# Attention with a Fourier mixer on one core: the round trip of batch 0 on another queue, and the last second products by blocks

## The chip, the core and the metric

The kernel runs on one core of one Trainium2 chip. The core has a matrix engine (TensorE, PE in the profile, with PEld for its weight loads), three engines for elementwise work (VectorE, DVE; ScalarE, ACT; GpSimd, POOL), and SyncE (SP), which here only issues transfers. Transfers can also be issued from the queues of ACT and of POOL. The metric is the time of one execution on the device, in microseconds (us).

## The reference

Inputs are q, k and v with 4 batches, 8 heads, 768 positions and 64 channels, and two weights, 512 x 2048 and 2048 x 512. What is computed, cut to what matters:

```python
scores = scale * q @ k.T - slope[h] * dist      # kept: the first 8 keys, and the last 96 keys
a = softmax(where(keep, scores, -1e9))
x = (a @ v), heads side by side                 # (4, 768, 512)
mixed = real(fft over positions, then over channels of x)
u = x + mixed
un = (u - mean(u)) / sqrt(var(u) + 1e-6)
out = u + maximum(un @ w_ch1, 0) @ w_ch2
```

## The kernel before

**Chunks.** Each batch has 768 rows, which come out of the Fourier mixer as six groups of 128 rows (row r, r + 6, ...). Two groups, a pair in `PAIRS`, make a chunk, so there are three chunks per batch and twelve in all (c = 0 to 11). Heads go in pairs (hp = 0 to 3).

**Attention.** `load` brings q, k, v of a head pair; for batches 0 and 1 they are cast (`cast_qk`, `cast_v0`) and transposed on PE (`trans`, tiles pt, copied out to qkT), and v is laid out by products with an identity (`v_place`, pvp). `score` makes the score bands (sc), ACT takes exp (ex), `v_global` and `glob` treat the eight global keys (pvg, pgl, eg), and `av` makes the weighted sums (pav), normalized by DVE into x.

**Bounce.** The residual needs x with its rows in the other grouping. `bounce` writes x to a scratch tensor in DRAM (xd) and reads it back as XR (xr). Batch 0 does it in two halves of the columns, and waits for both before the read. All of these transfers are issued from ACT's queue.

**Mixer.** `fold_3` (batch 0) or `fold_s` and `fold_d` combine rows and columns of x by symmetry on DVE; `y_unit` (py) is the transform over positions, `mirror` makes reversed copies on POOL (ww, rev), and `u_unit` (pu) is the transform over channels. DVE adds XR into u with the row sums (line 980), scales the sums to minus the mean (sm, line 984), and ACT or DVE makes un (lines 995, 997). `nt_unit` transposes un on PE (ptu), from chunk 7 on by a transposing transfer.

**The two products.** `ph_unit` makes one eighth of the first product of a chunk (16 blocks of 128, two at a time; 8 matmuls of 256 columns each), and ACT or DVE applies the maximum with 0 into hT. `pg_unit` makes a quarter of the second product for one row group t (4 matmuls of 512 columns), and after the fourth DVE scales it by the row's rstd and adds it to u, which SP stores.

**Who sets the order.** Nothing here is written out in order. The class `Plan` walks a model of the engines: every operation is given with what it needs, its cost and the engines that could do it; the planner places the earliest next, and picks from four streams of PE work (mixer, attention, ph, pg). What it emits is then each engine's fixed program. So a change of a need, a buffer, a bank or a queue moves other instructions too. Times on tokens for transfers are set in `Plan.emit`.

PSUM banks: two double banks "xx", and two more, C and D, that serve batches 0 and 1. When all users of C and D are done (the token CD), their space goes to the rings of ph and pg, two banks each. No ph can start before that. Weights are loaded by `wload` from POOL's queue, cast on the way, in eight pieces of 512 KB as stored. Before the first product there are twelve products of zeros (pz).

## Time and profile before

| | |
|---|---|
| median of 8 runs | 276.66 us (275.5 to 278.07) |
| profiled execution | 275.5 us |
| its span, first to last instruction | 273.7 us |
| mean granted clock of TensorE | 0.998 |
| PE, DVE, ACT, POOL busy | 257.1, 153.2, 148.6, 61.2 us |
| ph products (128x256) | 768, busy 94.3 us |
| pg products (128x512) | 384, busy 89.8 us |
| weight pieces, issue to landing (median) | 11.9 us |
| v of a head pair, issue to landing (median) | 7.3 us |
| writes xd of batch 0, issue to landing (median of four) | 7.0 us |
| read xr, issue to landing (median) | 4.7 us |

A row of the timeline gives the start, the duration, the engine, the line, the operation with output and inputs, how many, and in brackets the idle time before it and what ended it. Matmuls are pipelined, so that the duration of a group counts from the first start to the last end, and the pace of one is the distance from start to start. PEclk is the clock that TensorE was granted, in tenths. Where an engine waits for several things, the bracket names what came last.

### The profile page before, as it was taken

To read this page: it belongs to the slowest core of one execution; us is meant where nothing else is said; L and a number is where in the kernel's file an instruction comes from. 1 tells how busy PE (TensorE), PEld (TensorE's weight loads), DVE (VectorE), ACT (ScalarE), POOL (GpSimd) and SP (SyncE) were. 2 spreads that over 40 slices of the span, in tenths; PEclk is the share of its full clock that TensorE was granted. 3 is DMA by queue.
4 is the path that set the end of the run, shared out by engine and by line. 5 is a ranking of instruction groups with operands and counts; after the bars stand their busy time and mean duration, and the time that the engine had idled before them with its cause. 6 is when DMAs were issued, how large, how long until landed. Compare 5 with 4: busy or idle time off the path is not lost.

```text
span 273.7 us, 5973 instructions
## 1 busy us (share of the span) xinstructions
PE 257.1 (94%) x2420; PEld 171.1 (63%) x2420; DVE 153.2 (56%) x316; ACT 148.6 (54%) x257; POOL 61.2 (22%) x127
## 2 busy tenths in 40 slices
PE   8698899589789999999999999999999999999994
PEld 3344548459567864777486466568887677767441
DVE  4565954973885415665378968567896224211121
ACT  1486666594766633697772066998453263535000
POOL 1445195830002502413110023032004101010000
PEclk9999999999999999999999999999999999999999
DMA  7999999996935597968957994415341241210122
GB/s 205 291 293 312 351 271 232 207 198 124 261 118 170 126 156 169 234 140 140 220 137 181 179 327 93 106 38 41 84 150 41 77 79 40 77 41 31 48 77 78
DMA packets 75742, 42.01 MB, mean 153 GB/s; under 512 B 32834, under 2 KB 71746, under 8 KB 75714
## 3 DMA queue, kind: packets, MB, share of 16 engines
q1 hardware_dynamic: 66914, 31.14, 47.7%
q0 software_dynamic: 4224, 4.19, 9.3%
q10 hardware_dynamic: 4576, 6.29, 7.9%
q8 instruction: 19, 0.31, 0.5%
q14 instruction: 9, 0.07, 0.1%
HBM read 31.92 MB, written 9.44 MB: 151 GB/s over the span
## 4 chain that ended last, share of the span: by engine, by line
PE 76%; DVE 7%; SPq 5%; ACT 4%; DMA 3%; issue 2%; POOL 1%; ACTq 1%; DVEq 0%; POOLq 0%
PE pg L1087 30%; PE ph L1064 29%; PE py L881 5%; SPq L365 4%; PE pu L961 3%; PE sc L552 3%; PE pav L680 3%; DMA w<-in_q_dram 3%; ACT ex L575 2%; PE pav L669 1%; DVE sm L984 1%; DVE qkT L521 1%; ACT un L1004 1%; POOL ww L929 1%; PE ptu L1036 1%
## 5 line engine op out<-in xcount | busy, mean ns | idle before, releaser
L1064 PE MATMUL ph<-unT,w 128*128 128x256 f16 x768 | 94.3, 273 | 2.2 <-DVE hT L1071 2.2
L1087 PE MATMUL pg<-w,hT 128*128 128x512 f16 x384 | 89.8, 379 | 0.0
L1064 PEld LDWEIGHTS <-w 128*128 128x128 f16 x768 | 72.7, 98 | 19.1 <-issue 6.1
L1070 ACT ACTIVATE hT<-ph 128x512 f16<-128x512 f32 x75 | 44.8, 597 | 49.0 <-PE ph L1064 48.0
L1087 PEld LDWEIGHTS <-hT 128*128 128x128 f16 x384 | 36.9, 98 | 36.9 <-issue 0.8
L1096 DVE SCALAR_TENSOR_TENSOR u<-pg,sm,u 128x512 f32<-128x512 f32 x24 | 18.0, 750 | 57.2 <-PE pg L1087 57.1
L575 ACT ACTIVATE ex<-sc 128x992 f16<-128x992 f32 (+2 forms) x24 | 20.9, 926 | 13.9 <-PE sc L552 8.2
L1071 DVE TENSOR_SCALAR hT<-ph 128x512 f16<-128x512 f32 x21 | 14.5, 690 | 15.4 <-PE ph L1064 15.3
L572 ACT ACTIVATE er<-sc 128x992 f16<-128x992 f32 (+2 forms) x24 | 21.6, 924 | 1.6 <-PE sc L552 1.5
L1011 POOL TENSOR_SCALAR sm<-sm 128x2 f32<-128x2 f32 x12 | 3.1, 255 | 84.1 <-ACT un L1004 83.9
L369 ACT ACTIVATE qk<-qs 128x384 f16<-128x384 f32 (+1 forms) x31 | 14.5, 528 | 8.9 <-DMA qkT<-qk 8.5
L980 DVE SCALAR_TENSOR_TENSOR u<-pu,xr 128x512 f32<-128x512 f32 x24 | 15.6, 687 | 5.6 <-PE pu L961 2.9
L587 DVE TENSOR_TENSOR ex<-er,mk 128x992 f16<-128x992 f16 (+2 forms) x24 | 14.8, 626 | 5.2 <-ACT er L572 4.9
L552 PE MATMUL sc<-qkT 64*128 64x256 f16 (+1 forms) x192 | 17.1, 262 | 0.6 <-DVE qkT L521 0.6
L680 PE MATMUL pav<-v,ex 128*128 128x65 f16 x352 | 16.4, 193 | 1.0 <-ACT ex L575 1.0
L1004 ACT ACTIVATE un<-un 128x512 f16<-128x512 f16 x24 | 14.9, 621 | 3.9 <-DMA unT<-un 2.9
L680 PEld LDWEIGHTS <-ex 128*128 128x128 f16 x352 | 15.3, 97 | 2.3 <-issue 1.7
L929 POOL COPY ww<-zy 128x512 f16<-128x512 f16 x16 | 9.3, 611 | 31.2 <-PE py L881 31.2
L995 ACT ACTIVATE un<-u,sm 128x512 f16<-128x512 f32 x12 | 8.5, 717 | 14.0 <-DVE sm L984 11.0
L552 PEld LDWEIGHTS <-qkT 64*128 64x128 f16 x192 | 5.7, 94 | 14.9 <-issue 12.4
L481 POOL COPY kG<-qkT 64x8 f16<-64x8 f16 x32 | 9.5, 298 | 24.1 <-DMA qkT<-qk 13.3
L898 DVE CAST zy<-py 128x512 f16<-128x512 f32 (+1 forms) x9 | 8.3, 928 | 10.8 <-ACT zy L896 6.4
(103 smaller groups left out, 297.1 us busy)
## 6 DMA issues: line engine op xcount, KB each, us to landing
out_dram<-u SPq DMA_DIRECT2D x24, 256.0 KB, 2.0
w<-in_moe_w_ch_dram POOLq DMA_DIRECT2D x8, 512.0 KB, 11.9
qs<-in_q_dram SPq DMA_DIRECT2D x9, 384.0 KB, 4.4
qs<-in_k_dram SPq DMA_DIRECT2D x9, 384.0 KB, 5.2
u<-in_v_dram SPq DMA_DIRECT2D x8, 384.0 KB, 7.3
xr<-xd ACTq DMA_DIRECT2D x4, 768.0 KB, 4.7
qs<-in_v_dram SPq DMA_DIRECT2D x16, 192.0 KB, 3.9
w<-in_q_dram SPq DMA_DIRECT2D x4, 384.0 KB, 6.6
```

Of the source, the lines that this page charges most:

```text
L369: A(d, s, AF.Copy)
L552: nc.tensor.matmul(pa[:, s, c0:c0 + cw], TT[n][lo:lo + 64, 1, i * P:(i + 1) * P], TT[n][lo:lo + 64, 0, i * P:i * P + cw], start=(b > 1), s ...
L572: A(mine(), cut(pa), AF.Exp, 0.0, 0.125)
L575: A(cut(expst[hp][:, :, g * 512:g * 512 + (384 if g == 2 else 512)]), cut(pa), AF.Exp, 0.0, 0.125)
L587: VT(o, mine(), m, op=ALU.mult)
L680: nc.tensor.matmul(po[:, jj, hh * 65:(hh + 1) * 65], lhsT, v16[b % 2][:, i, h, 0:65], start=(jp == 0 and a == 0), stop=(a == len(ops) - 1) ...
L980: V.scalar_tensor_tensor(u[:, a].rearrange("p (n r) -> p n r", r=4), pu[:, a].rearrange("p (r n) -> p n r", r=4), 1.0, XR[b][:, rr].rearra ...
L1004: A(x, x, AF.Square, accum_out=MV[c][:, a, 2:3])
L1064: nc.tensor.matmul(ph[:, a * CH:(a + 1) * CH], W1[0][:, d, jb * P:(jb + 1) * P], UNT[c][:, d, :], start=(d == 0), stop=(d == ND - 1))
L1070: pl.later([("ACT", act(512), lambda: A(dst, ph, AF.Relu)), ("DVE", dve(512), lambda: V.tensor_scalar_max(dst, ph, 0.0))], [], e, [("h", c ...
L1087: nc.tensor.matmul(pg, HT[c][:, jb, t * P:(t + 1) * P], W2[0][:, jb, :], start=(jb == 0), stop=(jb == NJ - 1))
L1096: V.scalar_tensor_tensor(UT[c][:, t, :], pg, MV[c][:, t, 3:4], UT[c][:, t, :], op0=ALU.mult, op1=ALU.add)
```

## The change

- Batch 0's bounce is issued from SP's queue. The four v of batch 1 are loaded after its read has been issued (the token xi), three of them into the buffers qs.
- For batch 0, u is added by row group: each of the two adds is an operation of its own, and its row sum is scaled by ACT and not by DVE, so that un of one group does not wait for the other.
- The second product of chunks 8 to 11 is done by blocks of two by two. With the four blocks of hT (row group by half of the inner size) and of w2 (half of the inner size by half of the columns), sums of blocks are formed on DVE, and seven products of blocks take the place of eight. The sums over w2 are made once (`w2_sums`, into the buffers of the exps, after batch 3's last use of them), those over hT per chunk (`s_sums`, into the mask's buffer and in place). Seven blocks of 8 matmuls of 256 columns, and five adds to u, per chunk.
- Fourteen products of zeros follow the products of v of head pair 0, ten precede those of head pair 1.
- The weight pieces wait for the cast of k of batch 1's last head pair in place of v's second, and the planner's numbers for some landings are changed. The transpose of chunk 0 may use banks C and D.

```diff
+    LAND = {("xw", 0, 0): 33.0, ("xw", 0, 1): 37.0, ("xr", 0): 43.0}
...
-            self.tok[o] = end + lat if dma else (end + lat, eng)
+            self.tok[o] = max(end + lat, self.LAND.get(o, 0.0)) if dma else (end + lat, eng)
...
+    def vat(n):
+        return ("u", min(n, HP)) if n < HP or n == 2 * HP - 1 else ("qs", 2 + n - HP)
...
-            pl.later([("SP", 0.55, run)], free("u", n), 0.0, [("ld", n, 2)], lat=1.7, dma=1.45)
+            pl.later([("SP", 0.55, run)], free(*vat(n)) + [("xi",)] * (n >= HP), 0.0, [("ld", n, 2)], lat=1.7, dma=1.45)
...
+            idle = lambda k: [nc.tensor.matmul(pv[:, 1, 3 * P:4 * P], EG[:, 0:P], EG[:, 0:P], start=True, stop=True) for _ in range(k)]
+            if n == 1:
+                idle(10)
...
+            if n == 0:
+                idle(14)
...
-        on, eng = "ACT", nc.scalar
+        on, eng = ("ACT", nc.scalar) if b else ("SP", nc.sync)
...
+            def add1(a):
+                if a == 0:
+                    UT[c] = buf("u", HP + 1 + c, [P, 2, Dm], FP32, 2)
+                    MV[c] = wk.tile([P, 2, 4], FP32, tag="sm", name=f"sm_{c}", bufs=6)
+                V.scalar_tensor_tensor(UT[c][:, a].rearrange("p (n r) -> p n r", r=4),
+                                       pu[:, a].rearrange("p (r n) -> p n r", r=4), 1.0,
+                                       XR[b][:, PAIRS[pr][a]].rearrange("p (n r) -> p n r", r=4),
+                                       op0=ALU.mult, op1=ALU.add, accum_out=MV[c][:, a, 0:1])
...
+                for a in range(2):
+                    pl.later([("DVE", dve(512) + 0.06, lambda a=a: add1(a))],
+                             [("xr", b)] + (free("u", HP + 1 + c) if a == 0 else [("us", c, 0)]), e, [("us", c, a)],
+                             ([("free", "xr", b)] + CD(b, ring)) * a, ring=ring if a else None)
+                    pl.later([("ACT", 0.2, lambda a=a: A(MV[c][:, a, 1:2], MV[c][:, a, 0:1], AF.Copy, 0.0, -SC / Dm))],
+                             [("us", c, a)], 0.0, [("u", c, a)], rank=0)
...
+    def w2_sums(i):
...
+            VT(W2T(1)[:, k0], b22, b12, op=ALU.subtract)
+            VT(W2T(3)[:, k0], b12, b11, op=ALU.subtract)
+            VT(W2T(0)[:, k0], b22, W2T(3)[:, k0], op=ALU.subtract)
+            VT(W2T(2)[:, k0], b21, W2T(0)[:, k0], op=ALU.subtract)
...
+    def s_sums(c):
...
+        def s1():
+            VT(new(0), block(1, 0), block(1, 1), op=ALU.add)
+        def s3():
+            VT(block(1, 0), block(0, 0), block(1, 0), op=ALU.subtract)
+        def s2():
+            VT(new(1), SX[c, 0], block(0, 0), op=ALU.subtract)
+        def s4():
+            VT(new(2), block(0, 1), SX[c, 1], op=ALU.subtract)
...
+    def pg_units(c):
...
+        PG.append((h0 + ws, ("pg",), p1))
+        PG.append((h1 + [("s", c, 1)], ("pg",), p45))
+        PG.append(([("s", c, 2), ("ra", c, 0)], None, p6))
+        PG.append(([("s", c, 4), ("rd", c, 0)], None, p32))
+        PG.append(([("s", c, 3), ("ra", c, 1)], None, p7))
...
-            needs = [("vc", 5), ("free", "w1", 0)] if i == 0 else [("wl", 3), ("free", "w2", 0)] if i == 4 else [("wl", i - 1)]
+            needs = [("qk", 7, 1), ("free", "w1", 0)] if i == 0 else [("wl", 3), ("free", "w2", 0)] if i == 4 else [("wl", i - 1)]
...
+            if c >= CS:
+                s_sums(c)
+                pg_units(c)
+                continue
```

In `pg_units`, p1, p6 and p7 each make one block product into one bank (pgA), p45 and p32 two each into the other (pgD). Before p6 and p7 write pgA again, the add that reads it must be done (ra), and p32 waits in the same way for the add that reads pgD (rd).

## The prediction

> **What bounds the kernel now.** I read the page's busy shares and slices first, then the windows of 10 us, then the chain that ended last, and at each hole in TensorE the timelines of the engines that it waits for.

> ```profile
> PE 257.1 (94%) x2420; PEld 171.1 (63%) x2420; DVE 153.2 (56%) x316; ACT 148.6 (54%) x257; POOL 61.2 (22%) x127
> PE   8698899589789999999999999999999999999994
> PEclk9999999999999999999999999999999999999999
> ```

> TensorE (PE) is busy for 94% of the span at full granted clock; the low digits lie in the first third.

> ```profile
> 40.00:50.00 10.00, 9.10 (x117) 7.58 (x115) 5.07 (x9) 5.01 (x8) 6.89 (x12) 1.00 1.01 210
> 50.00:60.00 10.00, 7.51 (x122) 4.77 (x122) 8.54 (x21) 8.87 (x18) 5.36 (x11) 1.00 1.22 199
> 70.00:80.00 10.00, 7.82 (x57) 5.39 (x56) 8.74 (x16) 6.38 (x12) 0.00 (x0) 1.00 0.77 227
> 100.00:110.00 10.00, 10.00 (x56) 5.00 (x55) 4.53 (x10) 3.48 (x8) 2.05 (x5) 1.00 0.87 166
> ```

> Columns: stretch, length, busy time of PE, its weight loads, DVE, ACT, POOL, then clock, DMA share, GB/s. Summed over all windows PE lacks 12.9 us before 100 us, nothing between 100 and 260, and 3.7 us after its last product. So two things count: products taken away after 92 us come off the end one for one, and ahead of it only a hole in PE that closes counts.

> The last part of the chain (start, us, what):

> ```profile
> 243.07 1.75 PE ph L1064 x16
> 252.65 17.28 PE pg L1087 x80
> 269.95 0.75 DVE u L1096
> ```

> A pg product of 512 columns takes 17.28/80 = 0.216 us, a ph product of 256 columns 1.75/16 = 0.109. The end is pure PE work, one DVE add and a store.

> The holes, first at 25 to 30 us:

> ```profile
> 23.53 2.31 ACTq L719 DMA_DIRECT2D xd<-x  x2
> 25.89 2.56 ACT L575 ACTIVATE ex<-sc 128x992 f16<-128x992 f32 x3 [2.40 <-DVE vG L611]
> 26.94 0.34 PE L680 MATMUL pav<-v,ex 128*128 128x65 f16 x6 [0.48 <-ACT ex L575]
> 29.21 0.23 PE L669 MATMUL pav<-vG,eg 128*128 128x130 f16 x1 [0.35 <-ACT eg L645]
> ```

> ACT's queue spends 2.31 us issuing the first half of the bounce; the exps of head pair 3, whose scores lie ready, come late, and PE waits for the banks they hold. The name vG in the bracket is only the last semaphore; what held ACT is the line above. Next, at 48 us:

> ```profile
> 48.32 2.77 DVE L984 TENSOR_SCALAR sm<-sm 128x2 f32<-128x2 f32 x1
> 49.91 1.17 DVE L443 CAST v<-pvp 128x384 f16<-128x384 f32 x1
> 48.20 0.74 POOL L1183 DMA_DIRECT2D w<-in_moe_w_ch_dram  x1
> 48.94 0.62 POOL L929 COPY ww<-zy 128x512 f16<-128x512 f16 x1
> 49.49 0.74 POOL L1183 DMA_DIRECT2D w<-in_moe_w_ch_dram  x1
> 50.22 0.83 POOL L414 CAST er<-u 128x768 f16<-128x768 f32 x1
> 51.90 0.62 PE L1036 MATMUL ptu<-ident,un 128*128 128x128 f16 x8 [2.49 <-ACT un L995]
> ```

> The tiny sm scaling, 0.17 us elsewhere, takes 2.77 and ends at 51.09, as POOL's unbroken run does (51.05). un waits for it, and the transpose of un is what PE stands on.

> **The change, part by part.** I walk the instruction order of the changed kernel with durations of the one profiled execution. It took 275.5 us with a span of 273.7, so 1.8 lies outside; the median of the eight runs, 276.66, stands 1.2 above it. I sum against 275.5 and add the 1.2.

> *Block form (chunks 8 to 11).* Removed: 4 x 32 = 128 products of 512, 128 x 0.216 = 27.65 us. Added: 4 x 7 x 8 = 224 of 256, at ph's 0.109, 24.50. That is -3.15 on PE. The ph row already loads new weights for each 256 columns at this pace, so that is in the price. DVE gains per chunk four sums of 128x1024 (0.61 start to start at L750/L751) and three more adds, 4 x (2.4 + 1.5) = 15.6 us over the last 60 us, where DVE is busy 8 to 47%. The eight sums over w2 (8 x 0.61 = 4.9 us) go ahead of batch 3's last normalization and fold: from the last pav, sums 4.9, x 0.9, fold and zy 6.1, one add 0.7, g1 1.8, hence w ready 13.6 us later; ahead of py PE has 11 ph (9.6) and 6 quarter pg (5.2), 14.8. Hidden by 1.2 us; without that cover they would cost up to 4.9. At the very end, from the last ph product: relu to +0.75, two sums to +2.0, the add that frees a pg bank to +2.8, where PE wants it at +2.6. With semaphores, +0.3. The last add then waits 0.1 at most. Net -2.85. The bound above: all five products of chunk 11 wait in turn for a DVE step, some +2.

> *Batch 0's bounce on SP.* Its five issues leave ACT and follow t1x, whose issue ends at 29.44. The first half's issue (rows ready at 23.5) is then at 29.5, the second's when x is done, near 31.2. Landing of such writes is 3.9 to 7.5 us; without the four v loads beside them (6.44 us of issue at 29.54 in before) I take 4.5: 37. The read lands 4.2 to 4.9 later, 42, and its first user (u of chunk 0) comes at 44. On ACT, two qk casts (0.75 each) move in from POOL; still the exps of head pair 3 end near 27.4 in place of 28.35, and eg at 28.0 in place of 29.16. So pav_4_1 starts at 28.1, not 29.21: -1.1. The next qkT copies are earlier by 0.9, and the third goes to ACT, so that DVE has the last fold done at 36.4 in place of 38.2; the PE waits of 0.36 and 0.41 for qkT go. py starts near 36.8 (39.25), with one score group less ahead of it (0.84). PE's holes from 25 to 45 us: before 0.61 + 0.48 + 0.52 + 0.35 + 0.36 + 0.41 = 2.7, after about 1.0. That is -1.7.

> *v of batch 1 behind the bounce; weights earlier.* v4 to v7 are issued at 37.5 to 40 in place of 29.5 to 36; four pvp, their evacuations and all of batch 1's pav move back, and the first ph units come forward in their place, at about 52 (61.46 before). The eight weight issues come at about 36.8 to 43, in one run. Behind them on POOL stand the mirrors (ww, rev) and v's casts: eight by 0.75 ends near 43, rev at 44.7, where pu of chunk 1 needs it at 45.7; the last ww at 47, needed at 48. v4 must be in by 48. With xr (768 KB) and the four v sharing the DMA engines with the weights at half of some 290 GB/s (the rate from 10 to 20 us), v4 lands near 45, v7 near 53 (cast needed by 60). Nothing in before shows v beside weights: at best they land in 4 us, at worst after the last weight, 26 us behind the first issue as in before (39.8 to 66.1). I take the even split, for which the nearest row is xr itself, issued at 40.41 between the first weights and landed within 4.9.

> [...]

> *u by row groups.* The three sm scalings on DVE become six ACT scalings of 128x1 (nearest row: a 128x1 accumulator read, 0.19; up to 0.3 each; 1.2 to 1.8 us on ACT), and un of the first row group can start under the second's add. The 2.77 us stall has no instruction left to sit in.

> [...] But un on DVE is a tensor_scalar too and now comes at 47.3, in POOL's run of ww, kG and two casts (46.3 to 48.8). [...] I take 0.5.

> PE holes from 45 to 62: before 0.31 + 2.49 + 0.2 + 0.17 + 1.08 = 4.25. After: ph must wait until bank D's last user, pvp of v4, is evacuated behind ACT's squares and scalings (51.1 to 52.3, 1.2), 0.1 for ptu of chunk 2, 0.5 for the lock, 0.6 for v casts on POOL: 2.4. That is -1.8. What is late next is ACT, which from 48 to 61 has 12 us of work in 13.

> *70 to 92 us.* Before: 1.40 + 0.78 + 0.43 = 2.6, the first two waits for relus on DVE behind the fold while ACT does mk for 3.86 us. After, eight ph of chunk 0 are already done; ACT's mk comes in pieces, the relus have pg units beside them, py finds w ready 1 us early. I keep the mirror wait and some slack, 0.8: -1.8.

> *Zero products.* 14 x 0.057 = 0.8 us after pvp of v0, 10 x 0.057 = 0.6 before the next pvp: they fill the holes of 0.84 and 0.73 at 11.4 and 13.0. pt and sc there take the durations of later ones (0.83, 0.59), so there is no slow clock to cure: 0, between -0.1 and +0.2.

> **Sum.** -2.85 - 1.7 - 1.8 - 1.8 = -8.15. A walk by hand misses short waits; I add back 0.65, about the three shortest of before (0.31, 0.2, 0.17). -7.5: 268.0 for an execution like the profiled one, **269.2** against the median.

> **The rivals.**

> *Waits change places (0.20).* ACT and DVE are at 85 to 89% from 50 to 60 us and get ph's relus on top; the holes before 92 us only move and the block form alone is left: 276.66 - 2.85 = 273.8. For it speaks ACT's 12 us in 13; against it, that before leaves ACT idle for 23 of the first 60 us and the queue stall there goes for certain.

> *Nothing (0.08).* The w2 sums lose their 1.2 us of cover (copies 20% slower than L750) and the end waits for DVE three times: 3 us back, while the first part only moves: 276.4. The profile speaks for a busy DVE only from 140 to 160, not after 210.

> *v starves behind the weights, slower (0.12).* pvp of v4 stands in PE's order ahead of every ph. If the engines do not share evenly, v4 lands with the last weight, 36.8 + 26 = 63; with its cast and pvp PE goes on at 64 in place of 50: +14 - 7.5 = +6.5, 283.2. It decides from a landing at 56.5 on (7.5 us later than the 49 at which PE would feel it), that is 19 us after issue, where v took 7.3 in the median. For it: DMA share was above 1.2 through the weights from 46 to 64. Against: xr's 4.9.

> *No new waits at all (0.05).* Without my 2.2 us of allowances: 267.

> **How the numbers follow.** 0.55 for the sum, whose own range is 266.5 to 272, 0.20, 0.08, 0.12 and 0.05 as above. Faster by over 0.5% (1.4 us, about what a measurement of this kernel can tell): 0.55 + 0.20 + 0.05 = 0.80; within it 0.08; slower 0.12. The range of 266.3 to 276.6 leaves out the starved case and the best tail.

> **What would show it.** Right: 256 pg products of 512 columns in place of 384, and 224 of 256 columns at 0.109; no PE hole over 1.3 us between 25 and 92; no DVE scaling of 2 us; exps of head pair 3 without ACT's 2.4 us gap; xr landed before pu of chunk 0 ends; PE whole from 92 to the end but for 0.3. Wrong: PE standing at pvp of v4 or on ww/rev behind the weight issues; py of batch 3 waiting for DVE; PE waiting in the last 9 us for adds by more than 1 us.

## The result, and the profile after

The changed kernel takes 273.73 us (median of 20 runs, 270.62 to 276.72), the kernel before 276.85 in all runs (275.29 to 279.38). The medians give a gain of 3.1 us where 7.5 were forecast. The ratio is 0.9865, with a 95% interval of 0.9842 to 0.9887; it leaves out five runs that lie more than 1.5% above the fastest, and so stands for 3.7 us. The profiled execution took 273.71 us, with a span of 271.9.

Where the 4.5 us went is read in the same order as before. First the page's busy shares and slices:

```profile
PE 256.8 (94%) x2540; PEld 182.1 (67%) x2540; DVE 172.1 (63%) x349; ACT 153.3 (56%) x267; POOL 57.7 (21%) x123
PE   8798899679999899999999999899999999999994
PEclk9999999979999999999999999999999999999999
```

PE is as busy as before (256.8 and 257.1 us), though it has fewer products to make. The 7 near 70 us has become a 9. The eighth slice (47.6 to 54.4 us) has gone from 5 to 6 only, the ninth from 8 to 7, and in the ninth the granted clock falls to 7 tenths. The windows say how much (columns as before: stretch, length, PE, its weight loads, DVE, ACT, POOL, clock, DMA share, GB/s):

```profile
40.00:50.00 10.00, 10.00 (x122) 7.90 (x120) 5.81 (x14) 5.87 (x12) 6.75 (x15) 1.00 1.16 248
50.00:60.00 10.00, 5.66 (x63) 3.16 (x61) 4.55 (x10) 5.29 (x15) 2.53 (x4) 0.83 1.20 216
60.00:70.00 10.00, 9.40 (x121) 7.42 (x118) 3.02 (x5) 7.25 (x15) 2.53 (x4) 1.00 1.05 183
70.00:80.00 10.00, 10.00 (x148) 8.77 (x144) 7.84 (x16) 3.71 (x8) 2.39 (x3) 1.00 0.63 135
```

One window of 10 us lacks 4.34 us of PE and runs at 0.83 of the clock. PE's timeline in it:

```profile
50.84 0.36 PE L436 MATMUL pvp<-er,ident 64*64 64x128 f16 x12
56.14 0.40 PE L436 MATMUL pvp<-er,ident 64*64 64x128 f16 x12 [4.25 <-POOL er L420]
56.48 1.89 PE L1090 MATMUL ph<-unT,w 128*128 128x256 f16 x8
58.16 1.00 PE L553 MATMUL sc<-dist,sid 128*128 128x480 f16 x2
59.10 0.58 PE L563 MATMUL sc<-qkT 64*128 64x240 f16 x4
59.61 0.67 PE L1062 MATMUL ptu<-ident,un 128*128 128x128 f16 x8
60.12 1.91 PE L1090 MATMUL ph<-unT,w 128*128 128x256 f16 x16
...
67.22 0.36 PE L436 MATMUL pvp<-er,ident 64*64 64x128 f16 x12 [0.60 <-POOL er L420]
```

The products of v5 wait 4.25 us for POOL's cast, those of v7 0.60. The first ph stands behind those of v5 in PE's order, not only behind those of v4. Between the two waits eight ph take 1.89 us in place of 1.03, and two sc 1.00 in place of 0.58: the granted clock, 1.00 up to 56 us, is 0.59 from 56 to 58, 0.56 from 58 to 60, and 1.00 again from 60 on. From 56.14 to 60.12 stands work that takes about 2.45 us at full clock (each group at its usual pace), so some 1.5 us are lost on top. The casts on POOL say what they wait for:

```profile
49.96 0.82 POOL L420 CAST er<-qs 128x768 f16<-128x768 f32 x1 [2.11 <-DMA qs<-in_v_dram]
55.27 0.83 POOL L420 CAST er<-qs 128x768 f16<-128x768 f32 x1 [4.48 <-DMA qs<-in_v_dram]
60.89 0.82 POOL L420 CAST er<-qs 128x768 f16<-128x768 f32 x1 [3.70 <-DMA qs<-in_v_dram]
66.35 0.82 POOL L420 CAST er<-u 128x768 f16<-128x768 f32 x1 [3.58 <-DMA u<-in_v_dram]
```

So v4 to v7 land near 49.9, 55.2, 60.8 and 66.3, one about every 5.5 us. SP issued them from 38.17 on:

```profile
38.17 5.07 SPq L371 DMA_DIRECT2D qs<-in_v_dram  x3
43.29 6.20 SPq L371 DMA_DIRECT2D u<-in_v_dram  x1
```

All four issues had ended by 49.5, and v7 landed some 17 us after that. The DMA view for 44 to 60 us splits the two queues (packets, MB, share); q0 carries the weights from POOL, q1 carries v:

```profile
q0 software_dynamic: 2286, 2.26, 83.3%
q1 hardware_dynamic: 2292, 1.15, 35.3%
```

The packets are equal in number, 2286 and 2292, and unequal in size: 2.26 MB / 2286 is 989 bytes, 1.15 MB / 2292 is 502, both in the mean. In 16 us that is 141 GB/s for the weights and 72 for v. In every 3 us from 43 to 64 us the counts of the two queues lie within 3 of each other. So v's packets went through all the time, some 143 in each us (2292 in 16): what set v's landing behind 49.5 was not the late issue but this pace.

Most of the rest stands as forecast; a wait of 0.80 us at 173.73 (sc, for ACT) does not. ACT's exps of head pair 3 no longer stand behind the bounce:

```profile
24.45 0.98 ACT L586 ACTIVATE ex<-sc 128x992 f16<-128x992 f32 x1
...
26.06 1.66 ACT L586 ACTIVATE ex<-sc 128x960 f16<-128x960 f32 x2
```

They end at 27.7 (28.45 before). The 2.77 us of the sm scaling are gone, un on DVE takes 0.48 at 48.11 and 49.12, and xr is in before u needs it:

```profile
48.11 0.48 DVE L1023 TENSOR_SCALAR un<-u,sm 128x512 f16<-128x512 f32 x1
```

The end of the chain of waits is still pure PE, now with block products at 1.75 us for 16, which is the pace of the ph beside them:

```profile
251.06 1.75 PE ph L1090 x16
252.81 1.75 PE pgD L1194 x16
```

### The profile page after: what moved, and what is told of

Its sections match the earlier page's. It is cut to its first block, busy times and chain, and to the rows that moved or that the text cites. A ratio compares the mean times of both kernels' runs of the same rounds, so it can differ in the third digit from the quotient of the medians.

```text
span 271.9 us, 6257 instructions
## 1 busy us (share of the span) xinstructions
PE 256.8 (94%) x2540; PEld 182.1 (67%) x2540; DVE 172.1 (63%) x349; ACT 153.3 (56%) x267; POOL 57.7 (21%) x123
## 4 chain that ended last, share of the span: by engine, by line
PE 76%; DMA 13%; SPq 4%; DVE 2%; POOL 2%; issue 1%; ACT 1%; POOLq 0%; DVEq 0%
PE ph L1090 29%; PE pg L1113 21%; DMA u<-in_v_dram 11%; PE pgD L1194 5%; PE pav L690 4%; PE pgA L1194 4%; PE sc L563 3%; PE py L891 3%; SPq L371 3%; PE pu L971 3%; DMA xd<-x 2%; PE pav L679 1%; PE sc L558 1%; PE pt L526 1%; PE ptu L1062 1%
## 5 line engine op out<-in xcount | busy, mean ns | idle before, releaser
L1096 ACT ACTIVATE hT<-ph 128x512 f16<-128x512 f32 x75 | 44.6, 596 | 46.8 <-PE ph L1090 46.6
L1113 PE MATMUL pg<-w,hT 128*128 128x512 f16 x256 | 60.2, 379 | 0.0
L598 DVE TENSOR_TENSOR ex<-er,mk 128x992 f16<-128x992 f16 (+2 forms) x24 | 14.8, 626 | 12.0 <-ACT er L583 11.9
L375 ACT ACTIVATE qk<-qs 128x384 f16<-128x384 f32 (+1 forms) x33 | 15.4, 522 | 11.5 <-DMA qkT<-qk 8.4
L1122 DVE SCALAR_TENSOR_TENSOR u<-pg,sm,u 128x512 f32<-128x512 f32 x16 | 11.9, 747 | 8.8 <-PE pg L1113 8.8
L1030 ACT ACTIVATE un<-un 128x512 f16<-128x512 f16 x24 | 14.8, 620 | 1.0 <-DMA unT<-un 1.0
L1021 ACT ACTIVATE un<-u,sm 128x512 f16<-128x512 f32 x13 | 9.2, 719 | 10.6 <-DVE sm L994 10.5
L465 POOL CAST v<-qs 128x768 f16<-128x768 f32 x8 | 7.4, 928 | 35.8 <-DMA qs<-in_v_dram 35.8
L906 ACT ACTIVATE zy<-py 128x1024 f16<-128x1024 f32 (+1 forms) x11 | 9.0, 827 | 10.6 <-PE py L891 10.2
L990 DVE SCALAR_TENSOR_TENSOR u<-pu,xr 128x512 f32<-128x512 f32 x18 | 11.7, 687 | 4.3 <-PE pu L971 4.3
```

The lines of the kernel that those rows point to most:

```text
L375: A(d, s, AF.Copy)
L598: VT(o, mine(), m, op=ALU.mult)
L1030: A(x, x, AF.Square, accum_out=MV[c][:, a, 2:3])
L1096: pl.later([("ACT", act(512), lambda: A(dst, ph, AF.Relu)), ("DVE", dve(512), lambda: V.tensor_scalar_max(dst, ph, 0.0))], [], e, [("h", c ...
L1113: nc.tensor.matmul(pg, HT[c][:, jb, t * P:(t + 1) * P], W2[0][:, jb, :], start=(jb == 0), stop=(jb == NJ - 1))
```

## The experiments

**Issue v between the writes and the read.** The theory was that v is late because it lands beside the weights. This edit sends v before them; the rival was that the wait moves to xr.

```diff
-                      lat=1.7, dma=2.4 if b else 2.6)
+                      lat=1.7, dma=2.4 if b else 2.6,
+                      then=None if b or n == 0 else (lambda t: pl.tok.__setitem__(("xi",), pl.t["SP"])))
...
-        pl.later([(on, 0.5, rd)], ..., dma=3.8 if b else 2.4, then=None if b else (lambda t: pl.tok.__setitem__(("xi",), pl.t["SP"])))
+        pl.later([(on, 0.5, rd)], ..., dma=3.8 if b else 2.4)
```

> The four v of batch 1 are issued between the writes and the read of batch 0's bounce, where SP stands idle from 32.3 to 37.7 us and the DMA share falls to 0.12, and not behind the read. Theory (v shares the DMA engines with the weights and lands 12 to 23 us after issue; PE stands 4.25 us at a pvp, then runs some 4 us at half clock, and stands 0.6 us again): v lands by 40, no PE hole over 1.5 us from 45 to 70, clock 1.00 throughout; 6 us under the changed kernel, near 267. Rival (the waits only change place: xr now lands behind v, or ACT is the bound): u of chunk 0 waits for xr, and 3 us or less are gained, 271 or more.

Measured: 272.47 us (270.57 to 276.0), ratio 0.9812 [0.976, 0.9865]. The profiled execution is its slowest, 276.0. In it v4 is cast at 39.48, and no pvp waits; but xr, issued at 38.6 behind four v and now beside the weights, comes late. DVE's and PE's lines:

```profile
53.10 0.69 DVE L1000 SCALAR_TENSOR_TENSOR u<-pu,xr 128x512 f32<-128x512 f32 x1 [8.43 <-DMA xr<-xd]
```

```profile
54.32 0.96 PE L553 MATMUL sc<-dist,sid 128*128 128x480 f16 x2 [8.23 <-DVE v L454]
```

The name v in PE's bracket is only the next thing on DVE's queue; what DVE stood on is the line above. xr landed 14.4 us after its issue, where the changed kernel's took 5.7. v6, v7 and xr were issued on one queue, and its packets had v's size first: 419 packets with 0.21 MB, some 0.5 KB each, beside 426 of the weights from 43 to 46 us, and 72 with 0.30 MB, 4.2 KB each, from 49 to 52. So the read came in behind what was left of v when the weights began. In that execution the rival held, and the median too lies in its range (271 or more). The other five runs, from 270.57 up, have no profile.

**Fill the wait with products of zeros.** This asks what the slow clock cost (0.59 and 0.56 from 56 to 60 us).

```diff
+            if n == 5:
+                idle(68)
```

> The changed kernel with 68 more products of zeros of 128 columns (3.8 us) ahead of the second pvp of batch 1, where PE stands for 4.25 us; they end before v is there. Theory (the idle 4.25 us make the clock fall to half until 60 us): the same wait, but ph, sc and ptu from 56 to 60 take 2.45 us in place of 3.98: 1.5 us faster than the changed kernel, near 272.2. Rival (these products are slow because of transfers or of waits between them): no difference.

Measured: 273.62 us (273.0 to 275.29), ratio 0.989 [0.9848, 0.9933], the same as the changed kernel. The windows (PE, clock, DMA share, GB/s) show that the clock is held:

```profile
50.00:60.00 10.00, 9.57 (x148) 1.00 1.20 216
60.00:70.00 10.00, 8.10 (x105) 1.00 1.04 180
```

But v lands as late as ever, and the time comes back as longer waits:

```profile
61.58 0.36 PE L438 MATMUL pvp<-er,ident 64*64 64x128 f16 x12 [1.21 <-POOL er L420]
66.94 0.36 PE L438 MATMUL pvp<-er,ident 64*64 64x128 f16 x12 [0.69 <-POOL er L420]
```

The waits have grown by 1.3 us (1.90 in place of 0.60), nearly the 1.5 that the clock gave back. So the slow clock does not set the time here. What bounds this stretch is the landing of v7 near 66, which both kernels share.

**Read v in larger packets.** The two queues had 2286 and 2292 packets in the same 16 us. If they get equal packets at other sizes too, larger packets of v must bring it in early, with nothing else moved. The edit reads v of batch 1 with its positions in another order, so that the rows of one partition are contiguous, up to 3 KB; each engine's order is unchanged. What it leaves out is the reference's order of v, so the output is another one; the products have the same shapes.

```diff
-                run_dma(t, v, b, h0)
+                if b == 1:
+                    nc.sync.dma_start(t, v[b, h0:h0 + 2].rearrange("h s d -> (h s) d").rearrange("(p m t) d -> p m (t d)", p=P, t=2))
+                else:
+                    run_dma(t, v, b, h0)
```

> The changed kernel in the same order of instructions, but v of batch 1 is read so that each partition takes 12 rows that lie together (the positions land permuted, so the output is another one): packets of up to 3 KB in place of 512 B. Theory (software and hardware queues take turns by packet, 993 B of a weight against 512 B of v, so that v gets 71 of 216 GB/s): v gets more than half, lands within 4 to 8 us of issue, the 4.25 us wait and the slow clock go: 5 to 6 us faster than the changed kernel. Rival (shared by bytes, or the weights go first): v lands as late as now, no difference.

Measured: 269.63 us (268.23 to 270.93), ratio 0.9755 [0.9698, 0.9811]: 4.1 us less than the changed kernel (3.0 by the two ratios), somewhat under the 5 to 6 expected, and within 0.5 of the forecast of 269.2. The DMA view for 43 to 46 us, where both queues are loaded, here and below it in the changed kernel:

```profile
q1 hardware_dynamic: 254, 0.68, 63.2%
q0 software_dynamic: 254, 0.25, 49.0%
```

```profile
q0 software_dynamic: 425, 0.42, 82.5%
q1 hardware_dynamic: 426, 0.22, 34.8%
```

The packets are equal in number again, 254 and 254, but those of v now have 2.7 KB, and so v and what is left of xr get 0.68 MB of 0.93: 227 GB/s beside 83. In the changed kernel v got 0.22 MB of 0.64 in the same 3 us. q1 is nearly empty from 49 us on (17 packets to 52), no cast waits for v, and no pvp waits:

```profile
50.63 0.36 PE L439 MATMUL pvp<-er,ident 64*64 64x128 f16 x12
51.64 0.36 PE L439 MATMUL pvp<-er,ident 64*64 64x128 f16 x12
52.70 1.03 PE L1093 MATMUL ph<-unT,w 128*128 128x256 f16 x8 [0.70 <-ACT v L458]
```

**Without the block form.**

```diff
-    CS = 8
+    CS = 12
...
-        for i in range(2):
+        for i in range(2 if CS < 12 else 0):
             w2_sums(i)
```

> The changed kernel with the second product of chunks 8 to 11 as before (no block products, no sums). Theory (block form is worth 3.15 us on PE less 0.3 of waits at the end): 2.85 us slower than the changed kernel, near 276.6, level with before. Rival (DVE's sums and waits eat it): less than 1 us slower.

Measured: 276.75 us (271.57 to 278.84), 3.0 above the changed kernel in the medians. It is a weak measurement: the runs spread over 7.3 us, though their order up to 180 us is that of the changed kernel. The profiled one is the fastest, and there v happened to be issued faster (5.7 us for the four in place of 11.3) and 874 packets of q1 were through from 40 to 43 us, where the changed kernel's profile has 147 (two executions of two kernels that agree up to there). v is cast at 48.14, 50.25, 55.73 and 61.18, with one pvp wait of 0.30. That suggests that with v issued beside the weights its landing varies from execution to execution; one execution of each does not show it. A clean size of the block form needs a base without that.

**Put the weights behind v5 again.** The first weight waits for v5's cast, as it did before the change.

```diff
-            needs = [("qk", 7, 1), ("free", "w1", 0)] if i == 0 else ...
+            needs = [("vc", 5), ("free", "w1", 0)] if i == 0 else ...
```

> One edit against the changed kernel: the weight pieces wait again for the cast of v5 (as in the kernel before), so v4 and v5 land before any weight is issued. Theory 'v starves beside the weights': v4 to v7 land about as fast as in the kernel before (7 us), no pvp waits over 1 us, the clock stays full, and the time comes to 268.5 to 270.5 (the 269.6 of the run with large packets). Rival 'the weights then come too late': the first pieces are issued near 45 to 49 us in place of 37 to 43, the mirrors and casts stand on POOL behind the waits for v, and PE stands at py, pu or at ph for w1 instead: 272 to 274, no gain over 273.7.

Measured: 271.58 us (269.99 to 273.55), ratio 0.9842 [0.9794, 0.9889]. What the theory said of v held: it takes 7.0 us in the median and the weights 9.9, no pvp waits, the clock stays at 1.00. Its number (268.5 to 270.5) was missed by 1.1. The profiled execution, the fastest, still has a ph wait of 1.18 us for u at 57.48, and near 168 us three waits of 2.3 in all, where the changed kernel has one of 0.8; what the slower five executions lose is not profiled, nor why the six spread over 3.6 us.

**Both: v in the gap, weights behind v5.** The first edit needs xr free of the weights, the fifth gives it that.

The edits are those of the first and the fifth, together:

```diff
+                      then=None if b or n == 0 else (lambda t: pl.tok.__setitem__(("xi",), pl.t["SP"])))
...
+            needs = [("vc", 5), ("free", "w1", 0)] if i == 0 else ...
```

> Two edits: v of batch 1 is issued between the writes and the read of the bounce (as in e1), and the weight pieces wait for the cast of v5 (as in e5). SP stands idle there for about 5 us for the writes, so v costs the queue nothing, and the read meets fewer weights than in e1. Theory: v lands by 41 to 44, the read (issued near 38.6) by 45 to 46, no wait over 1 us is left in 45 to 65: 268 to 270. Rival: the read, issued behind four v, meets v6, v7 and the first weights, lands after 48 and u waits for it: 271 to 273.

Measured: 269.14 us (268.93 to 269.45), ratio 0.9737 [0.97, 0.9773]. Not only is it the fastest, its six runs lie within 0.52 us of each other, where those of the changed kernel spread over 6. SP sends v in the time in which it would only wait for the second half of x, and POOL's casts and first weights follow at once:

```profile
33.22 3.29 SPq L371 DMA_DIRECT2D qs<-in_v_dram  x3
36.56 1.06 SPq L371 DMA_DIRECT2D u<-in_v_dram  x1
37.80 1.07 SPq L738 DMA_DIRECT2D xr<-xd  x1
```

```profile
38.79 0.82 POOL L420 CAST er<-qs 128x768 f16<-128x768 f32 x1 [1.55 <-DMA qs<-in_v_dram]
40.05 0.83 POOL L420 CAST er<-qs 128x768 f16<-128x768 f32 x1 [0.44 <-DMA qs<-in_v_dram]
40.81 3.18 POOL L1345 DMA_DIRECT2D w<-in_moe_w_ch_dram  x4
```

xr lands 6.7 us after its issue, at 44.5, and u begins at 44.87 without waiting for it. Two waits of PE over 1 us are left all the same, 1.10 at 49.29 and 1.23 at 58.13, where none was expected; the time is in the range expected.

**On the base with large packets: no block form, and the bounce on ACT.** The first repeats the edit of the fourth experiment; the second, with the token xi taken from ACT's time in place of SP's, is:

```diff
-        on, eng = ("ACT", nc.scalar) if b else ("SP", nc.sync)
+        on, eng = "ACT", nc.scalar
```

> The base is the kernel of e3 (v of batch 1 read in packets of up to 3 KB, so its positions are in another order than the reference's), where v does not vary; on it the block form of chunks 8 to 11 is undone. By the working of the prediction (3.15 on PE less 0.3 at the end): 269.6 + 2.85 = 272.5, and the time from 180 us to the end longer by that. If the block form is worth its matmuls alone, 272.8; if the waits for DVE cost 1 us or more, under 271.8.

Measured: 270.82 us (270.38 to 272.39), ratio 0.9808 [0.9766, 0.9851], only 1.2 above its base, which ran on another chip, where 2.85 were expected. Its profiled execution, span 270.6, is 4.2 longer than that of the base (266.4); 1.5 of that is lost between 90 and 100 us (PE 7.72 in place of 9.23), where the block form plays no part. The base varies by more than the term in question: inconclusive.

> The base is the kernel of e3 (v of batch 1 read in another order of positions); on it batch 0's bounce is issued from ACT's queue again. If the row of the prediction holds, ACT stands for about 2.3 us in the issue of the first half, the exps of head pair 3 come late, and PE loses 1.7 us from 25 to 45: 271.3. Rival: the writes then start at 23.5 in place of 30, xr is in early, the v loads follow it earlier, and what is lost at 25 to 30 comes back by 65: 269.0 to 270.2.

Measured: 272.95 us (271.24 to 274.48), ratio 0.9874 [0.9828, 0.992], 3.3 above the base (which ran on another chip). The direction is that of the prediction, and the size is not local to ACT: from 20 to 40 us PE loses only 0.66 against the base (17.71 and 18.37 busy). The rest comes later. The edit also moved v: its issue starts at 30.05 and not at 37.68. The second writes go out at 33.15, just behind v (the four writes land 7.6 us after their issue in the median, 5.4 in the changed kernel), and the read, issued only at 42.15, stands beside the weights, issued from 37.03 to 43.70; DVE waits for it until 50.28:

```profile
50.28 0.69 DVE L1002 SCALAR_TENSOR_TENSOR u<-pu,xr 128x512 f32<-128x512 f32 x1 [5.20 <-DMA xr<-xd]
```

PE stands 3.82 us there. The prediction had priced the bounce's place by what it blocks on ACT; what counts more is when its read comes.

**On the steady base: again, no block form, joint u, no zeros.** The kernel of the sixth experiment has the spread that small terms need. Four kernels on one chip: itself again, the block form undone, u of batch 0 joint again, and the 24 products of zeros left out.

```diff
-            if b:
+            if True:
                 pl.later([("DVE", 2 * dve(512) + 0.25, add)], ...
```

```diff
-                idle(10)
+                pass
...
-                idle(14)
+                pass
```

> The kernel of e6 again, as the base of the three that follow on the same chip: 269.1, within 0.3, since nothing in it waits for a transfer that varies.

> On the kernel of e6, whose runs lie within 0.5 us, the block form of chunks 8 to 11 is undone. By the working of the prediction the time rises by 2.85 (3.15 on PE less 0.3 of waits at the end), to 272.0; by the matmuls alone by 3.15; by the medians of the kernels of e3 and e7, whose spreads are wider, by 1.2 only, and then the sums and adds on DVE must cost nearly 2 us that the profile of the changed kernel does not show at its end.

> On the kernel of e6, u of batch 0 is added and scaled for both row groups together again, by three scalings on DVE. If the stall of the 128x2 scaling beside POOL (2.77 us in the kernel before) comes back, PE waits for un once by about 2 us near 48, and the time is 270.5 to 271.5. If what POOL does at that moment is a weight issue or nothing, it costs what un comes later, 0.5 at most: 269.1 to 269.6.

> On the kernel of e6, the 24 products of zeros around the products of v of head pairs 0 and 1 are left out. By the prediction they fill holes and change nothing: within 0.2 of e6. If they hold the clock up, the products behind them run at half speed without them, about 1 us: 270.1.

| kernel | median us | range | ratio to before | against the base |
|---|---|---|---|---|
| the base again | 269.21 | 268.51 to 269.41 | 0.9726 [0.9692, 0.9761] | |
| no block form | 271.58 | 270.75 to 271.9 | 0.9815 [0.9783, 0.9848] | +2.37 |
| u joint | 270.69 | 270.28 to 272.11 | 0.9797 [0.9762, 0.9832] | +1.48 |
| no zeros | 269.12 | 268.61 to 270.2 | 0.9731 [0.9697, 0.9764] | -0.09 |

*Block form: 2.37 us.* From the ph at 83.15 to the end of the last product the base takes 180.5 us, and without the block form, from 83.12, 183.1: 2.57 of PE; after it the base takes some 0.15 longer to the end of the span. The steps from start to start in the base show where the difference to 3.15 lies:

```profile
217.46 1.04 PE L1195 MATMUL pgA<-w,hT 128*128 128x256 f16 x8
218.47 1.03 PE L1195 MATMUL pgD<-ex,hT 128*128 128x256 f16 x8
219.34 1.04 PE L1195 MATMUL pgD<-ex,mk 128*128 128x256 f16 x8
...
256.02 1.04 PE L1195 MATMUL pgA<-ex,hT 128*128 128x256 f16 x8
257.24 1.03 PE L1195 MATMUL pgA<-w,hT 128*128 128x256 f16 x8 [0.18 <-DVE u L1213]
258.11 1.04 PE L1195 MATMUL pgD<-ex,hT 128*128 128x256 f16 x8
```

The usual step is 0.87. It is 1.01 at 217.46 and 1.22 at 256.02 (and 1.01 again at 259.85): 0.14 + 0.35 + 0.14 = 0.63 lost, not 0.3. Each of the three late products starts 0.05 to 0.06 us after an add to u on DVE ends (218.41, 257.19 and 260.80), so these are waits for DVE, though the row names it only once.

*u by row groups: 1.48 us.* With the joint form the long scaling is back (0.17 us for the same line at 52.27), beside POOL:

```profile
46.40 2.76 DVE L995 TENSOR_SCALAR sm<-sm 128x2 f32<-128x2 f32 x1
```

It ends at 49.16; POOL runs from 44.19 without a gap, and its cast of v6 ends at 49.14. PE stands 1.93 us until 49.24, by the row for DVE's cast of v, which follows that scaling on DVE's queue. The price of the wait was well read, and the median is at the lower end of what was expected from it.

*Zeros: nothing*, as forecast. Without them PE waits 0.84 and 0.77 us in their place.

## Why the prediction was off

**The step that failed** is the landing of v in "v of batch 1 behind the bounce": "I take the even split", which put v4 near 45 and v7 near 53. It came out at 49.9 and 66.3; what held the first ph was v5, at 55.2. The issue, forecast to end by 40, ended at 49.5. The even split was the author's estimate, with nothing in before to show v beside the weights, and it meant equal bytes. The runs show equal packets (2286 and 2292 in 16 us), and v's have 502 bytes in the mean against 989: 72 GB/s of 213, in place of half of 290. Both factors were wrong, the share and the total. The total could have been read in the windows of before, which move 210 and 199 GB/s beside the weights; the 290 came from 10 to 20 us, with no weights. The nearest row was badly chosen as well: xr's 4.9 us was no evidence for v, since the trace of before gives xr's queue 144 packets for 0.79 MB, 5.5 KB each. With packets equal in number such a read moves most of the bytes: in the changed kernel, from 41 to 42 us, xr's queue had 47 packets and 0.29 MB beside 46 and 0.05 of the weights. v, at 502 bytes a packet, got 72 of 213 GB/s, a third.

**What it cost.** PE's holes from 45 us on were forecast at 2.4 and are 4.25 + 0.60, with about 1.5 of slow clock: 6.35. Of the 2.4, little was needed (in the run with large packets ph waits 0.70 where 1.2 was set, and un and the casts cost nothing). The error is thus near 4 us. The run with large packets, which changes v's landing and nothing in the order, gives 4.1 back by the medians, 3.0 by the ratios, and 5.5 between the two profiled executions (273.71 and 268.23). The zeros in the wait show no price of the slow clock by itself, as far as two medians 0.1 apart can tell; what sets the stretch is v7. The starved rival had the right direction at a wrong size: it gave v nothing until the last weight, where v got a third of the bytes.

**The terms one by one.**

- Block form, -2.85: -2.37 on the steady base. The products were right at 0.109 each; the waits for DVE are 0.63 and not 0.3, and the tail is some 0.15 longer. The sums over w2 cost nothing, as argued: py of batch 3 runs without a wait. The cover was thinner than stated, though: the parts listed (4.9, 0.9, 6.1, 0.7 and 1.8) add up to 14.4 and not 13.6, which leaves 0.4 of 14.8.
- Bounce off ACT, -1.7: PE's waits from 25 to 45 us are 0.74 + 0.19 + 0.53 = 1.5, where 1.0 was forecast (2.7 before), so about -1.2. (The exps before end at 28.45 by their row, not 28.35.) py starts at 37.45, not 36.8. The return to ACT costs 3.3, but mostly by the late read, so it does not size this term.
- u by row groups, inside the -1.8 for 45 to 62: right in direction, 1.48 by itself on the steady base. The 0.5 "for the lock" in the sum is a term that no run shows. What the runs showed in its place: in the changed kernel un on DVE took 0.48 at 48.11 and 49.12, when POOL stood idle (47.85 to 49.96) because v was late; on the steady base it took 1.59, starting as POOL's mirror does (46.83):

```profile
46.78 1.59 DVE L1024 TENSOR_SCALAR un<-u,sm 128x512 f16<-128x512 f32 x1
```

  The mirror ends at 47.45 and un only at 48.37, within POOL's next cast. So un took 1.59 beside POOL's mirror, weight issue and cast here, and 0.48 beside a weight issue in before (51.12); what set the 1.59 was not shown.

- 70 to 92 us, -1.8: the mirror wait (for ww, at 97.64) and one for a relu on DVE (at 90.97) remain,

```profile
90.97 1.03 PE L1090 MATMUL ph<-unT,w 128*128 128x256 f16 x8 [0.78 <-DVE hT L1097]
97.64 0.95 PE L971 MATMUL pu<-t,ww 128*128 128x128 f16 x14 [0.49 <-POOL ww L939]
```

 1.3 us in place of 0.8, so about -1.3.
- Zeros, 0: right.

With +2.1 for 45 to 67 in place of -1.8, these add up to -2.4 - 1.2 - 1.3 + 2.1 = -2.8. Two losses stand in no term: by 22 us the changed kernel is 0.4 late (its pvp at 22.71, before at 22.30), and there is the wait of 0.80 at 173.73, where before has none. That makes -1.6, near the 1.8 by which the two profiled executions differ (275.5 and 273.71). The medians differ by 3.1, because the profiled execution of before lies 1.35 under its median and that of the changed kernel lies at its own.

**Luck.** The rival "waits change places" named 273.8, and 273.73 was measured. Its cause was not the one: ACT and DVE, which it had full, are busy for 5.29 and 4.55 of the 10 us from 50 to 60. Still, its outcome is close to what happened, since the loss of 2.1 eats most of the gains of 1.2 and 1.3 and the block form is what is left. That the kernel of large packets met 269.2 owes something to terms that cancel: smaller gains, and allowances of 0.5 and 0.6 that were not needed.

## What to carry to other kernels

Where two queues share the DMA engines, compare packet sizes before bytes: here v, at 502 bytes a packet, got 72 of 213 GB/s beside weights at 989, and at 2.7 KB a packet its queue got 227 of 310. A load with packets as small as v's that must land in time was better off ahead of the prefetch than beside it (269.14 us in place of 273.73). Look for a queue that merely waits (SP before the second half of x) and put the urgent load there; then hold the prefetch by a real wait (a cast that needs the load's data, ahead of it on its queue), not by an estimate of when things land. And size small terms on a base whose runs agree: the same edit read +3.0 and +1.2 on bases that vary, and +2.4 on the one that does not.
